# One Trainium2 core, linear attention beside a state-space convolution: two-bank PSUM tiles in neighbouring banks, position zero inside the spectrum, another issue order

## The chip, the core and the metric

The kernel runs on one core of a Trainium2 chip. Five engines work side by side, each through a queue of its own that it takes in order: PE (TensorE, matmuls and transposes; its weight loads have a row of their own, PEld), DVE (VectorE), ACT (ScalarE), POOL (GpSimd) and SP (SyncE, which here only issues DMA transfers). Work passes from engine to engine through on-chip memory: SBUF, and PSUM, into which PE writes, in eight banks of 512 float32 numbers for each of 128 partitions. The metric is the device time of one launch in microseconds (us), the median of several runs.

## The reference

Two branches on 2048 positions, 448 columns each, written side by side. The first is linear attention with 16 heads of 28 columns, in which softmax features of the projected query and key stand for the usual score matrix. The second is a state-space layer: a kernel K of length 2048 for each column, summed over 256 complex states, convolved with u, plus a skip term.

```python
# A: x [1,2048,448], wqkv [448,1344], w_phi [16,28,28], wo [448,448]
q, k, v = heads(x @ wqkv)
phi(t)  = concat(softmax(t @ w_phi), softmax(-t @ w_phi))
kv = einsum("bhsf,bhsd->bhfd", phi(k), v);  z = einsum("bhsf->bhf", phi(k))
o  = phi(q) @ kv / (phi(q) @ z + 1e-6)
a  = merge_heads(o) @ wo
# B: u [1,2048,448], A, B, C complex [448,256], log_dt, Dskip [448]
dt = exp(log_dt)
K  = einsum("dn,dnl,dn->dl", C, exp(dt * A * l), dt * B).real     # l = 0..2047
y  = irfft(rfft(u, 4096) * rfft(K, 4096))[:2048] + u * Dskip
out = concat([a, y], -1)
```

## The kernel before

The code first records 1127 operations, in the order in which a reader would write them, and then issues them in another order, which is a list of numbers, `ORDER`. An operation is a group of matmuls, or one instruction of another engine, or a DMA; `prog.add(engine, fn)` records it. A framework puts in the waits: an instruction waits for the earlier ones (in the order of issue) that touch the same memory, as far as the views that they are given tell. The stages, as recorded:

- **Loads, states, powers.** `to_states` spreads dt·A and C·B over the states by matmuls; CR is the product of C, B and dt. Tables of powers (PW) follow from exponentials, sines and squares. `flip_x` transposes x by PE into xT; `fold_weights` multiplies the key and query weights by w_phi.
- **signal_spectrum(b)**: matmuls of u with a table of constants; the result goes to DRAM (SUd) and comes back, piece by piece, for the convolution.
- **rotations, dampings, hi_tables(qt)**: for a quarter qt of the columns, arguments of sines and exponentials by matmuls into a pair of banks (`args`), then ACT, then DVE products into tables.
- **key_side**: 16 tiles of 128 positions. Each takes two projections of four matmuls (banks 4 and 5 in the code as written), two exponentials, a copy of the values (all ACT), a reduction, a reciprocal and a product (DVE), and eight matmuls that add the tile to kv and z, in a bank for each sign that stays taken through all 16 tiles (`bK`). The sets of buffers alternate between two.
- **tables(qt)**: `damp` and `far` products on DVE, and `build_k`, small matmuls that sum K over the states; K goes to DRAM (KTd) and comes back in another layout.
- **query_side(sc)**: a quarter of the positions: projections, exponentials, denominators; the scale factors go to DRAM (SCd), are read back spread over the partitions, and are multiplied into the features (EQ); then the output matmuls.
- **kernel_spectrum_pair, kernel_spectrum, conv(qt)**: the spectrum of K by matmuls with constant tables, products with the signal's spectrum on DVE (pieces of SUd come by POOL's queue into one buffer), and inverses of 36 matmuls each, whose results ACT copies out and SP stores.

Banks are handed out by a second list: the n-th `prog.take("P", ...)` gets the n-th entry of `SLOTS`, one digit for one bank, two for a pair. Of the 44 two-bank jobs, 28 have banks that are not neighbours (such as "07", "17", "26"). One of them is the argument tile of `rotations(0)` that the rows below show at 75.12: "17". A pair is read by one instruction with one view, whose step is the distance of the banks:

```python
    def two(bs, parts=128):
        return view(psum[0:parts, bs[0], 0:1], [512 * (bs[1] - bs[0]), 2], [1, D_MODEL])
```

K at position zero needs no powers: it is the sum of CR over the states. Before, matmuls of CR with a matrix of ones give that sum, the same on all partitions, and DVE adds it to DSK (the Dskip row, spread over the partitions), so that the skip term carries it.

Each engine's helper functions have one line each, which is what the profile names: `tt` L159 (DVE tensor_tensor), `smul` L171, `stt` L174, `vcopy` L177, `recip` L184, `af` L187 (ACT activation), `acopy` L190 (ACT copy), `mset` L193, `mms` L198 (matmuls), `transposes` L208, `dma` L213; the reduction of `key_side` is L592.

Of the kernel before, what the change touches and what calls it, by code (L numbers as in the profile page):

```python
# [102 lines left out]
def kernel(  # L103
# [117 lines left out]
    HM = sb(3200, [112, 4, D_HEAD + 1])  # L221
    bias_hp = sb(3440, [128, 1], F32)
# [123 lines left out]
    mset(ones, 1.0)  # L346
    dma("G", DSK, bass.AP(tensor=B_Dskip.tensor, offset=B_Dskip.offset, ap=[[0, 128], [1, D_MODEL]]))
# [5 lines left out]
    add(DSK, DSK, psum[:, bs[0], 0:D_MODEL])  # L353
# [72 lines left out]
    dma("G", HM, M_d)  # L426
    dma("G", wo, A_wo.rearrange("(c p) n -> p c n", p=112))
# [150 lines left out]
    def key_side():  # L578
        bK = prog.take("P", 6), prog.take("P", 7)
# [104 lines left out]
    def spectrum_terms(o, ft, b, rhs, sk0, m, cp):  # L684
        n = len(TERMS[b])
        items = [(o, ft[:, cp, fi, :], rhs(kt), dict(start=(k == 0), stop=(b == 0 and k == n - 1)))
                 for k, (fi, kt) in enumerate(TERMS[b])]
        if b == 1:
            items.append((o, (NEG, ident)[cp], sk0(1 - cp, m), dict(start=False, stop=True)))
        return items  # L690

    def kernel_spectrum_pair():
        tiles = {}

        def spec(m, b):
            (bk,) = prog.take("P", 4 + b)
            items = []
            for cp in range(2):
                items += spectrum_terms(
                    view(psum[:, bk, QC * cp:QC * cp + 1], [112, 2], [1, 112]), tiles[m], b,  # L700
                    lambda kt: view(KT[0][:, kt, 0:1], [672, 2], [1, 112]),
                    lambda c, k: view(SK[0][:, 0, c, k // 4, k % 4, 0:1], [3584, 2], [1, 112]), m, cp)
            mms(items)
            for g in range(2):
                acopy(SK[g][:, b, :, m // 4, m % 4, :], view(psum[:, bk, 112 * g:112 * g + 1], [QC, 2], [1, 112]))
# [7 lines left out]
    def kernel_spectrum(qt, tiles, banks):  # L713
        sk = SK[qt % 2]
        for m in range(0, 8, 2):
            for b in range(2):
                (bk,) = prog.take("P", banks[b])
                items = []
                for cp in range(2):
                    for k in range(2):  # L720
                        at = 112 * (2 * cp + k)
                        items += spectrum_terms(
                            psum[:, bk, at:at + 112], tiles[m + k], b, lambda kt: KT[qt % 2][:, kt, :],
                            lambda c, i: sk[:, 0, c, i // 4, i % 4, :], m + k, cp)
# [152 lines left out]
).split()]  # L877
SLOTS = [[int(c) for c in i] for i in (
# [33 lines left out]
```

## Time and profile before

| | |
|---|---|
| Median of 3 runs | 332.09 us (331.78 to 334.99) |
| Profiled execution, its own time | 335.36 us |
| Its span, first to last instruction | 333.4 us |
| Mean granted PE clock, as a share of full speed | 0.887 |
| DMA | 35.73 MB, 107 GB/s |

The rows below are from the one profiled execution; their times count from the span's start. In rows of the timeline the bracket holds the idle time of that engine just before the instruction, and what ended it.

### The profile page before, as it was taken

To read this page: it belongs to the slowest core of one execution; us is meant where nothing else is said; L and a number is where in the kernel's file an instruction comes from. 1 tells how busy PE (TensorE), PEld (TensorE's weight loads), DVE (VectorE), ACT (ScalarE), POOL (GpSimd) and SP (SyncE) were. 2 spreads that over 40 slices of the span, in tenths; PEclk is the share of its full clock that TensorE was granted. 3 is DMA by queue.
4 is the path that set the end of the run, shared out by engine and by line. 5 is a ranking of instruction groups with operands and counts; after the bars stand their busy time and mean duration, and the time that the engine had idled before them with its cause. 6 is when DMAs were issued, how large, how long until landed. Compare 5 with 4: busy or idle time off the path is not lost.

```text
span 333.4 us, 8578 instructions
## 1 busy us (share of the span) xinstructions
PE 249.7 (75%) x3741; PEld 186.4 (56%) x3741; DVE 267.5 (80%) x325; ACT 205.6 (62%) x340; POOL 15.6 (5%) x31
## 2 busy tenths in 40 slices
PE   2846698896699857787967577997995608979595
PEld 2735444454355544564543375647785608879595
DVE  4286958891899988696987887999996799989990
ACT  4889548887877784866847866696544421424231
POOL 7310000000000000000010000000000000100000
PEclk9975769999999985699978989999996967979899
DMA  7999105330200000042645061787509354486022
GB/s 213 253 204 237 30 2 159 111 112 0 89 23 0 0 2 1 2 89 72 122 85 234 2 168 22 157 276 247 138 4 314 74 83 168 151 210 117 0 57 58
DMA packets 51341, 35.73 MB, mean 107 GB/s; under 512 B 32008, under 2 KB 47384, under 8 KB 50920
## 3 DMA queue, kind: packets, MB, share of 16 engines
q1 hardware_dynamic: 48328, 27.90, 34.1%
q0 software_dynamic: 2976, 7.28, 7.1%
q8 instruction: 29, 0.48, 0.6%
q14 instruction: 8, 0.07, 0.1%
HBM read 26.30 MB, written 8.85 MB: 105 GB/s over the span
## 4 chain that ended last, share of the span: by engine, by line
PE 37%; DVE 28%; DMA 15%; ACT 13%; issue 4%; SPq 2%; DVEq 0%; ACTq 0%
PE psum L198 36%; DVE sbuf L159 22%; ACT sbuf L187 7%; DMA sbuf<-in_A_x_dram 5%; DMA sbuf<-in_B_C_re_dram 4%; ACT sbuf L190 4%; DMA sbuf<-SCd 4%; DVE sbuf L592 4%; SPq L213 2%; DVE sbuf L184 1%; DMA sbuf<-const 1%; ACT L187 1%; DMA SCd<-sbuf 1%; PE psum L208 0%; DVE sbuf L177 0%
## 5 line engine op out<-in xcount | busy, mean ns | idle before, releaser
L198 PE MATMUL psum<-sbuf 128*16 128x48 bf16 (+10 forms) x3632 | 237.7, 265 | 63.3 <-ACT sbuf L187 21.5
L159 DVE TENSOR_TENSOR sbuf<-sbuf 128x896 bf16<-128x896 bf16 (+13 forms) x235 | 219.5, 975 | 32.9 <-ACT sbuf L187 16.3
L198 PEld LDWEIGHTS <-sbuf 128*16 128x16 bf16 (+4 forms) x3632 | 175.3, 112 | 125.9 <-issue 70.4
L190 ACT CAST sbuf<-psum 128x448 bf16<-128x448 f32 (+4 forms) x140 | 75.4, 570 | 77.3 <-PE psum L198 70.1
L187 ACT ACTIVATE sbuf<-psum 128x448 bf16<-128x448 f32 (+4 forms) x140 | 83.9, 659 | 33.0 <-PE psum L198 31.7
L208 PE MATMUL psum<-sbuf 128*112 128x128 bf16 (+3 forms) x109 | 13.0, 305 | 16.4 <-DMA sbuf<-in_A_x_dram 7.3
L187 ACT ACTIVATE sbuf<-psum,sbuf 128x896 bf16<-128x896 f32 (+3 forms) x28 | 21.7, 807 | 2.5 <-PE psum L198 2.1
L208 PEld LDWEIGHTS <-sbuf 128*112 128x112 bf16 (+3 forms) x109 | 11.6, 207 | 17.0 <-DMA sbuf<-in_A_x_dram 8.0
L592 DVE TENSOR_REDUCE sbuf<-sbuf 128x32 f32<-128x896 bf16 x16 | 17.2, 1080 | 1.3 <-ACT sbuf L187 1.2
L177 DVE COPY sbuf<-psum 112x1024 bf16<-112x1024 bf16 (+2 forms) x16 | 7.6, 475 | 12.8 <-PE psum L208 8.6
L187 ACT ACTIVATE sbuf<-sbuf 128x896 bf16<-128x896 bf16 (+3 forms) x13 | 11.5, 901 | 8.5 <-DVE sbuf L159 7.6
L187 ACT ACT_TABLE_LOAD x11 | 14.1, 1283 | 0.9 <-PEq L896 0.7
L171 DVE TENSOR_SCALAR sbuf<-sbuf 128x3584 bf16<-128x3584 bf16 (+4 forms) x11 | 6.7, 607 | 2.1 <-PE psum L198 1.6
L184 DVE RECIPROCAL sbuf<-sbuf 128x32 bf16<-128x32 f32 (+1 forms) x20 | 7.8, 392 | 0.6
L213 POOL DMA_DIRECT2D sbuf<-SUd x4 | 2.1, 531 | 114.2 <-DVE sbuf L159 114.2
L213 POOL DMA_DIRECT2D sbuf<-const x3 | 1.7, 569 | 114.2 <-PE psum L198 114.2
L213 POOL DMA_DIRECT2D sbuf<-in_B_u_dram x8 | 6.4, 808 | 12.2 <-PE psum L208 12.2
L159 DVE TENSOR_TENSOR sbuf<-psum,sbuf 128x128 f32<-128x128 f32 (+3 forms) x10 | 4.7, 493 | 2.0 <-ACT sbuf L187 1.3
L190 ACT COPY sbuf<-psum 112x896 bf16<-112x896 bf16 x5 | 4.3, 919 | 2.3 <-PE psum L208 2.3
L190 ACT CAST sbuf<-sbuf 128x1792 bf16<-128x1792 f32 x3 | 5.1, 1691 | 0.0
L159 DVE TENSOR_TENSOR sbuf<-sbuf,psum 112x448 bf16<-112x448 bf16 (+1 forms) x2 | 1.2, 621 | 4.3 <-issue 3.4
L174 DVE SCALAR_TENSOR_TENSOR sbuf<-sbuf 128x64 f32<-128x64 f32 (+1 forms) x6 | 3.0, 506 | 0.0
(12 smaller groups left out, 9.5 us busy)
## 6 DMA issues: line engine op xcount, KB each, us to landing
sbuf<-const SPq DMA_DIRECT2D x16, 384.0 KB, 4.2
SUd<-sbuf SPq DMA_DIRECT2D x8, 448.0 KB, 4.8
sbuf<-SCd SPq DMA_DIRECT2D x16, 224.0 KB
sbuf<-SUd POOLq DMA_DIRECT2D x4, 896.0 KB, 6.2
sbuf<-const POOLq DMA_DIRECT2D x2, 1024.0 KB, 6.0
sbuf<-in_A_x_dram SPq DMA_DIRECT2D x4, 448.0 KB, 5.1
out_dram<-sbuf SPq DMA_DIRECT2D x4, 448.0 KB
sbuf<-in_B_u_dram SPq DMA_DIRECT2D x16, 112.0 KB, 4.2
```

The costliest lines, as they stand in the source:

```text
L159: prog.add("V", lambda: nc.vector.tensor_tensor(out=o, in0=a, in1=b, op=op))
L171: prog.add("V", lambda: nc.vector.tensor_scalar_mul(o, a, s))
L174: prog.add("V", lambda: nc.vector.scalar_tensor_tensor(out=o, in0=a, scalar=s, in1=b, op0=op0, op1=op1))
L177: prog.add("V", lambda: nc.vector.tensor_copy(o, a))
L184: prog.add("V", lambda: low(lambda: nc.vector.reciprocal(o, a)))
L187: prog.add("A", lambda: nc.scalar.activation(o, a, fn, **kw))
L190: prog.add("A", lambda: nc.scalar.copy(o, a))
L198: nc.tensor.matmul(o, lhsT=l, rhs=r, **kw)
L208: nc.tensor.transpose(o, i, idn)
L213: prog.add(eng, lambda: e.dma_start(out=o, in_=i))
L592: prog.add("V", lambda zk=zk, EK=EK: nc.vector.tensor_reduce(zk, EK.rearrange("p s (h f) -> p s h f", f=D_HEAD), axis=AX.X, op=ALU.add))
```

## The change

Three things change. First, both banks of a two-bank tile are now neighbours: `SLOTS` holds only the pairs 01, 12, 23, 34, 45, 56 and 67, and `key_side` takes its two accumulation banks as one such pair. Secondly, K at position zero becomes part of K's spectrum: the matrix of ones is filled with 2^-17 in place of 1, ACT copies the summed row to a new tile K0, and the real part of the spectrum for b = 0 gets one more matmul, with a table column block of ones, W[:, 0, 31, 0:128], and K0; that is 24 matmuls, 8 of them of 224 columns and 16 of 112. DVE's add goes, and DSK is loaded later on POOL's queue. Thirdly, `ORDER` and `SLOTS` are new from end to end.

```diff
+    K0 = sb(86016, [128, D_MODEL])
...
     ones = sb(212544, [128, 128])
-    mset(ones, 1.0)
-    dma("G", DSK, bass.AP(tensor=B_Dskip.tensor, offset=B_Dskip.offset, ap=[[0, 128], [1, D_MODEL]]))
+    mset(ones, 2.0 ** -17)
     bs = prog.take("P", 0)
     mms([it for qt in range(4) for it in acc(
...
-    add(DSK, DSK, psum[:, bs[0], 0:D_MODEL])
+    acopy(K0, psum[:, bs[0], 0:D_MODEL])
...
     dma("G", HM, M_d)
+    dma("G", DSK, bass.AP(tensor=B_Dskip.tensor, offset=B_Dskip.offset, ap=[[0, 128], [1, D_MODEL]]))
     dma("G", wo, A_wo.rearrange("(c p) n -> p c n", p=112))
...
     def key_side():
-        bK = prog.take("P", 6), prog.take("P", 7)
+        bk_ = prog.take("P", 6, 7)
+        bK = bk_[0:1], bk_[1:2]
...
-    def spectrum_terms(o, ft, b, rhs, sk0, m, cp):
-        n = len(TERMS[b])
-        items = [(o, ft[:, cp, fi, :], rhs(kt), dict(start=(k == 0), stop=(b == 0 and k == n - 1)))
-                 for k, (fi, kt) in enumerate(TERMS[b])]
+    def spectrum_terms(o, ft, b, rhs, k0, sk0, m, cp):
+        pairs = [(ft[:, cp, fi, :], rhs(kt)) for fi, kt in TERMS[b]]
         if b == 1:
-            items.append((o, (NEG, ident)[cp], sk0(1 - cp, m), dict(start=False, stop=True)))
-        return items
+            pairs.append(((NEG, ident)[cp], sk0(1 - cp, m)))
+        elif cp == 0:
+            pairs.append((W[:, 0, 31, 0:128], k0))
+        return acc(o, pairs)
...
 SLOTS = [[int(c) for c in i] for i in (
-    "0 12 34 0 26 34 6 0 4 3 7 0 7 0 7 0 6 5 07 07 26 34 02 34 02 67 34 67 7 0 34 26 02 02 23 67 17 23 17 17 23 "
...
+    "0 23 67 0 67 23 7 0 1 2 0 4 5 4 6 4 5 5 45 23 01 56 01 67 23 23 23 67 2 2 45 56 67 01 01 67 23 67 67 23 67 "
...
```

The new order shows best on the queues themselves. DVE where the key side begins, in the kernel before: the products of 1792 and 3584 columns make the power tables and CR's products with them, TENSOR_REDUCE, RECIPROCAL and the product of 928 belong to a key tile, and the row that reads psum is the add into DSK.

```order
L159 TENSOR_TENSOR sbuf<-psum,sbuf 128x896
L159 TENSOR_TENSOR sbuf<-sbuf 128x1792
L159 TENSOR_TENSOR sbuf<-sbuf 128x896
L159 TENSOR_TENSOR sbuf<-sbuf 128x1792
L159 TENSOR_TENSOR sbuf<-sbuf 128x3584
L592 TENSOR_REDUCE sbuf<-sbuf 128x32
L159 TENSOR_TENSOR sbuf<-sbuf 128x896
L184 RECIPROCAL sbuf<-sbuf 128x32
L159 TENSOR_TENSOR sbuf<-sbuf 128x896
L159 TENSOR_TENSOR sbuf<-sbuf,psum 128x448
L174 SCALAR_TENSOR_TENSOR sbuf<-sbuf 128x896
L159 TENSOR_TENSOR sbuf<-sbuf 128x928
```

The same place of DVE's queue after the change, from the last power tables on; COPY from psum to 112x2x4x128 is a piece of xT, and the products of 112 rows are those of B and C.

```order
L159 TENSOR_TENSOR sbuf<-sbuf 128x1792
L159 TENSOR_TENSOR sbuf<-sbuf 112x1024 x2
L159 TENSOR_TENSOR sbuf<-sbuf 128x1792
L594 TENSOR_REDUCE sbuf<-sbuf 128x32
L184 RECIPROCAL sbuf<-sbuf 128x32
L159 TENSOR_TENSOR sbuf<-sbuf 128x928
L594 TENSOR_REDUCE sbuf<-sbuf 128x32
L184 RECIPROCAL sbuf<-sbuf 128x32
L159 TENSOR_TENSOR sbuf<-sbuf 128x928
L159 TENSOR_TENSOR sbuf<-sbuf 128x1792
L177 COPY sbuf<-psum 112x2x4x128
L594 TENSOR_REDUCE sbuf<-sbuf 128x32
```

Three key tiles now stand where one stood, ahead of CR's products of 3584 columns, and there is no add that reads psum.

SP's queue, the loads of the opening, in the kernel before; in_A_x is x in four pieces, in_A_wqkv the query and key weights (896 columns) and then the value weights (448), in_B the other branch, and const 128x4096 a table of constants.

```order
L213 DMA sbuf<-in_A_x_dram 128x1792
L213 DMA sbuf<-in_A_wqkv_dram 112x4x896
L213 DMA sbuf<-in_B_A_im_dram 112x4x256
L213 DMA sbuf<-in_B_B_im_dram 112x4x256
L213 DMA sbuf<-const 128x4096
L213 DMA sbuf<-in_A_x_dram 128x1792
L213 DMA sbuf<-in_B_u_dram 64x4x448 x2
L213 DMA sbuf<-in_B_B_re_dram 112x4x256
L213 DMA sbuf<-in_B_C_im_dram 112x4x256
L213 DMA sbuf<-in_A_x_dram 128x1792 x2
L213 DMA sbuf<-in_A_wqkv_dram 112x4x448
```

The same stretch of SP's queue after the change.

```order
L213 DMA sbuf<-in_A_x_dram 128x1792
L213 DMA sbuf<-in_B_A_im_dram 112x4x256
L213 DMA sbuf<-in_A_wqkv_dram 112x4x896
L213 DMA sbuf<-in_A_x_dram 128x1792
L213 DMA sbuf<-in_B_B_im_dram 112x4x256
L213 DMA sbuf<-in_A_x_dram 128x1792
L213 DMA sbuf<-in_B_u_dram 64x4x448 x2
L213 DMA sbuf<-in_A_wqkv_dram 112x4x448
L213 DMA sbuf<-in_B_C_im_dram 112x4x256
L213 DMA sbuf<-in_B_C_re_dram 112x4x256
L213 DMA sbuf<-in_B_B_re_dram 112x4x256
```

Three pieces of x and the value weights now come ahead of three of the four loads of B and C, and the table of 4096 columns follows behind them; on POOL's queue, the four loads of w_phi, which stood ahead of all pieces of u, now stand between them.

## Rows read from the trace of the kernel before

**Rows 1.** The page: busy time of each engine, and the chain that ended last.

```profile
PE 249.7 (75%) x3741; PEld 186.4 (56%) x3741; DVE 267.5 (80%) x325; ACT 205.6 (62%) x340; POOL 15.6 (5%) x31
...
PE 37%; DVE 28%; DMA 15%; ACT 13%; issue 4%; SPq 2%; DVEq 0%; ACTq 0%
```

**Rows 2.** Stages: length, busy time of each engine, granted clock, DMA share, GB/s.

```profile
0.00:35.50 35.50, 19.70 (x153) 16.49 (x154) 20.27 (x21) 26.89 (x29) 11.14 (x21) 0.81 1.01 220
35.50:84.80 49.30, 40.71 (x256) 23.28 (x255) 34.28 (x43) 36.45 (x51) 1.20 (x4) 0.90 0.21 67
84.80:121.20 36.40, 31.27 (x219) 18.60 (x217) 34.62 (x41) 28.99 (x54) 0.00 (x0) 1.00 0.07 24
121.20:207.00 85.80, 62.76 (x1212) 44.03 (x1212) 68.38 (x97) 57.95 (x95) 1.11 (x2) 0.84 0.30 76
207.00:324.80 117.80, 90.70 (x1822) 79.53 (x1815) 109.92 (x124) 53.76 (x110) 2.12 (x4) 0.90 0.53 142
324.80:333.40 8.60, 4.61 (x94) 4.44 (x91) 0.00 (x0) 1.60 (x3) 0.00 (x0) 1.00 0.26 56
```

**Rows 3.** Waits of the whole span: total us, times, longest.

```profile
PE psum L198 <- ACT sbuf L187: 21.5, 17, 4.8
...
DVE sbuf L159 <- ACT sbuf L187: 17.6, 5, 6.6
PE psum L198 <- ACT sbuf L190: 15.6, 18, 2.3
...
DVE sbuf L159 <- DMA sbuf<-SUd: 3.2, 1, 3.2
```

**Rows 4.** Timeline from 73 to 81: start, busy time, instruction, idle before it.

```profile
75.12 0.92 ACT L187 ACTIVATE sbuf<-psum 128x896 bf16<-128x896 f32 x1 [0.28 <-PE psum L198]
...
76.08 2.44 PE L198 MATMUL psum<-sbuf 112*128 112x448 bf16 x16 [1.00 <-ACT sbuf L187]
```

**Rows 5.** DVE's timeline of the opening.

```profile
17.40 3.96 DVE L159 TENSOR_TENSOR sbuf<-sbuf 128x1792 bf16<-128x1792 f32 x2 [5.92 <-ACT sbuf L187]
...
27.39 2.30 DVE L159 TENSOR_TENSOR sbuf<-sbuf 112x1024 bf16<-112x1024 bf16 x3 [1.84 <-DMA sbuf<-in_B_C_im_dram]
...
44.33 1.08 DVE L592 TENSOR_REDUCE sbuf<-sbuf 128x32 f32<-128x896 bf16 x1
...
50.10 0.62 DVE L159 TENSOR_TENSOR sbuf<-sbuf,psum 128x448 bf16<-128x448 bf16 x1 [3.42 <-issue]
```

**Rows 6.** DMA, 0 to 40 us: busy tenths in 40 slices; issues, us to landing.

```profile
DMA  0069999999999999999999999999999999500000
...
sbuf<-in_B_u_dram POOLq DMA_DIRECT2D x8, 112.0 KB, 13.1
...
sbuf<-in_A_w_phi_dram POOLq DMA_DIRECT2D x4, 6.1 KB, 4.9
```

**Rows 7.** SP's queue from 138 to 160: issues of transfers.

```profile
141.26 0.34 SPq L213 DMA_DIRECT2D SCd<-sbuf  x1
144.85 1.70 SPq L213 DMA_DIRECT2D sbuf<-SCd  x4
```

**Rows 8.** DVE's timeline from 140 to 172.

```profile
152.88 2.36 DVE L159 TENSOR_TENSOR sbuf<-sbuf 112x2048 bf16<-112x2048 bf16 x2 [2.40 <-DMA sbuf<-SCd]
```

**Rows 9.** Timeline from 322 to the end.

```profile
320.30 4.48 DVE L159 TENSOR_TENSOR sbuf<-sbuf 128x3584 bf16<-128x3584 bf16 x6
...
329.50 0.53 ACT L190 CAST sbuf<-psum 128x448 bf16<-128x448 f32 x1 [1.29 <-PE psum L198]
```

**Rows 10.** Groups by shape: busy us, mean ns, idle before.

```profile
L198 PE MATMUL psum<-sbuf 128*128 128x112 bf16 x808 | 47.3, 226 | 11.8 <-ACT sbuf L187 5.8 <-DVE sbuf L159 3.5 <-issue 2.0
...
L190 ACT CAST sbuf<-psum 128x448 bf16<-128x448 f32 x64 | 33.4, 538 | 42.0 <-PE psum L198 35.1 <-DVE sbuf L159 4.5 <-issue 1.8
```

**Rows 11.** Two stretches of 20 us, columns as in rows 2.

```profile
20.00:40.00 20.00, 13.32 (x108) 10.98 (x109) 16.15 (x19) 15.43 (x15) 1.88 (x3) 0.59 0.83 161
...
100.00:120.00 20.00, 18.27 (x137) 11.54 (x135) 18.93 (x26) 15.79 (x32) 0.00 (x0) 1.00 0.00 1
```

More of the change, by code (lines that the diff above doesn't have):

```diff
@@ L700, in spec @@
                     view(psum[:, bk, QC * cp:QC * cp + 1], [112, 2], [1, 112]), tiles[m], b,
-                    lambda kt: view(KT[0][:, kt, 0:1], [672, 2], [1, 112]),
+                    lambda kt: view(KT[0][:, kt, 0:1], [672, 2], [1, 112]), view(K0[:, 0:1], [112, 2], [1, 112]),
                     lambda c, k: view(SK[0][:, 0, c, k // 4, k % 4, 0:1], [3584, 2], [1, 112]), m, cp)
@@ L723, in kernel_spectrum @@
                             psum[:, bk, at:at + 112], tiles[m + k], b, lambda kt: KT[qt % 2][:, kt, :],
+                            K0[:, 112 * qt:112 * qt + 112],
                             lambda c, i: sk[:, 0, c, i // 4, i % 4, :], m + k, cp)
```

94 rows, old and new, of tables (ORDER, SLOTS) are left out of this document.

## The prediction

> **What bounds the kernel now.** I read the page's busy shares and chain first, then each engine's busy time by stage, then who waits for whom, and last the places in the timeline where those waits stand. DVE is busy 267.5 of 333.4 us, PE 249.7, ACT 205.6, and the chain that ended last passes through all of them: PE 37%, DVE 28%, DMA 15%, ACT 13% [rows 1]. No engine is full over the whole span; the kernel loses time where engines hand work over. The stages show where [rows 2]. DVE sits idle 15.2 us of the first 35.5 (loads and power tables), 15.0 of the next 49.3 (first part of the key side), only 1.8 of the 36.4 in which the key side ends, 17.4 of 85.8 (tables and query side), 7.9 of 117.8 (spectra and convolution), and all of the last 8.6. That is 65.9 us; a better order or fewer waits can take back that and no more, unless it also cuts DVE's work.
>
> Some of the handovers are between instructions that share no data. At 75.12 ACT starts on the two-bank argument tile of `rotations(0)`, which lies in banks 1 and 7. It started, after 0.28 us of idle time, when signal_spectrum's matmuls ended, though these write banks 2 and 3; and PE's value projection of key tile 2, into bank 4, stood 1.00 us until ACT was through [rows 4]. The view of banks 1 and 7 is one stepped pattern, and what lies between them is waited for as if it were read. 28 of the 44 two-bank jobs had such a pair. Matching each wait of the trace with the banks in `SLOTS`, I count 47 in which the engine that ended last shares no bank with the one that waits, 57.6 us of local idle time, 38.6 of it ACT's and 16.6 PE's. Most of that is no loss of the kernel: what counts is what reaches DVE, for which the grouped waits give 17.6 us behind ACT, while PE stands 21.5 and 15.6 us behind ACT [rows 3].
>
> **The change part by part.**
>
> *Opening, to 35.5 us.* The DMA engines are full from 2 to 35 us [rows 6], and nothing is loaded less, so the loads' own waits stay: at DVE 5.92 us before 17.40 and 1.84 us before 27.39 [rows 5]. DVE's first key-tile reduction stands at 44.33 there [rows 5]; the new order puts x and the value weights ahead on SP's queue and the reductions right behind the power tables, so they fill some of the 15.2. I take 11 us of idle as left, between 7.8 (these two waits alone) and 15.2: −4.2.
>
> On POOL's queue the four loads of w_phi go between pieces of u. Here they took a median of 4.9 us and the eight pieces 13.1 [rows 6], so the last may land 8.2 us later; PE's folding of weights waits for it, and the first projection of a key tile for that. With x only partly there by then I take nothing for it, 8.2 as the far end. The rows say that transfers of this size take their time while all engines are full. The Trainium skill, page "DMA: Bandwidth & Descriptors", section "Issuing engines are not separate DMA queues", says that transfers share the 16 engines whoever issues them, and that several issuers save only issuing time; by it the new places on POOL's queue would change less than the 8.2, and the sum not at all.
>
> *Key side.* Of 85.7 us DVE is idle 16.8 [rows 2]. The false handovers lie here above all: `rotations`, `dampings`, `signal_spectrum` and `hi_tables` use pairs between the key tiles. In the second half, where DVE has table work between tiles, it is idle 5% (1.78 of 36.40). If that holds for the whole 85.7, 4.2 are left; I take 5.0, so −11.8 (ends: 0 and −15). About 18 us of table work that stood ahead of the last key tile now stands behind it; it is moved, not removed, and makes the middle denser.
>
> *Position zero.* DVE's add into DSK goes: 0.62 us, after 3.42 idle that lie in the key side's 15.0 already [rows 5]. So −0.6. In its place ACT copies 128x448 from PSUM, 0.538 us a piece [rows 10]; ACT is idle 12.9 us of that stretch [rows 2], so zero, 0.5 at most. PE gets 24 matmuls: 16 of 112 columns at 226 ns, and 8 of 224 which I price alike from below and at twice that from above: 5.4 to 7.2 us [rows 10]. PE is idle 27.1 us in the last working stage [rows 2]; without that cover all would count. I take 0.7, an eighth, as reaching DVE. DSK's load moves behind others and is needed only for the final adds: zero.
>
> *Middle, 121.2 to 207.* DVE waits here for chains that go around it. One is the store of the query side's factors to DRAM and its reload: store issued at 141.26, loads issued from 144.85, DVE's multiply at 152.88 [rows 7, 8], 11.6 us. In the new order the DVE work that stands between is 9 to 11.7 us for each of the four, so most is covered, with 7 to 9 us of idle time left for the four with shortfalls, queueing behind other transfers, and the transposes ahead of them; squares on ACT add 1 to 3. Of 17.4 I keep 11.4: −6.0 (ends −2 and −9).
>
> *Convolution.* One buffer takes each next piece of signal spectrum. DVE stood 3.2 us for one of them [rows 3]. It remains one buffer, so 1.5 us twice, and 2.4 for tables of constants: 5.4 of 7.9 stay, −2.5 (ends 0 and −4).
>
> *Tail.* DVE ends at 324.78, when PE still has three inverses of 36 matmuls in its queue, one every 1.8 us (ACT stands idle 1.29 before it copies one out in 0.53); ACT's last copy is at 329.50 and takes 0.53, and the last store ends the span at 333.40 [rows 9]. In the new order one inverse depends on, and stands behind, DVE's last instruction: 1.8 + 0.53 + 3.4 (from 330.03 to 333.40) = 5.7; with 0.2 of handovers 5.9, not 8.6: −2.7 (ends −3.6 and 0, as PE may still be behind).
>
> **Sum:** −4.2 −11.8 −0.6 +0.7 −6.0 −2.5 −2.7 = −27.1. The profiled execution took 335.36, so 308.3; the median of the timed runs lies 3.27 below it (332.09): 305.
>
> **The rivals.**
>
> *B, DVE alone decides.* If interleaving keeps it fed, its busy time, 267.5 − 0.6 = 266.9, plus loads 7.8, tail 5.9 and the two DMA waits of [rows 3, 8] (3.2 + 2.4 = 5.6) give a span of 286; less 1.3, which is how the median stands to the span, 285. For it: DVE at 95% in one stage already. Against: PE and ACT each have over 200 us and their chains must then never come late.
>
> *C, the key side stays an interlock.* Its −11.8 falls away, the rest holds: 317. For it: two projections, two exponentials, a copy, a reduction, a reciprocal, a multiply and eight matmuls follow each other through three engines with two sets of buffers, which the change leaves alone. Against: the second half already does it at 95%. A pair now has only seven places, so it may wait truly for a bank where it waited falsely before. The Trainium skill, page "Perfetto Trace Analysis", section "Matmuls", says that independent groups of matmuls should go round different banks, so that one is emptied while the next is filled; by it fewer places for pairs cost time, and the outcome would be this one. No row separates the two, as both look like PE waiting for ACT.
>
> *Nothing reaches the path.* The waits removed were off it, and a new order brings waits of its own as long: 332, give or take 3.3.
>
> *D, slower: the clock.* PE's granted clock in 20 to 40 us was 0.59, near the lower of its two levels (1.2 of 2.4 GHz), after a stretch in which PE waited for loads; from 100 to 120 it was 1.00 [rows 11]. If short matmul groups separated by DVE-paced gaps hold it at 0.59 through the key side, the 72.0 us that PE was busy there at 0.94 (mean of [rows 2]) become 115; that stage ends at 35.5 + 115 = 150.5 in place of 121.2, and +29 against the −4.2 −0.6 +0.7 −6.0 −2.5 −2.7 of the rest gives 346. It decides from a mean clock of about 0.65, at which PE's time there is 104 and eats what the rest brings. Against: the new order has fewer waits between PE's groups, and 0.90 and 1.00 were held with more. The Trainium skill, page "TensorE: Matmul & The Clock Gate", section "Part 1: The HAM clock gate", says the slow state is the default and activity lifts it; the trace agrees in its 0.59 and 1.00, and whether gaps of the new kind suffice no row shows.
>
> **How the numbers follow.** Forecast 0.52 (296 to 313), B 0.14 (285 to 296), C 0.20 (313 to 324), nothing 0.06, D 0.08. Leaving out D, nothing and the lower half of B gives 290 to 324 for the range. A measurement of this kernel tells about 1% (3.3 us) from no change: faster 0.86, same 0.06, slower 0.08.
>
> **What would show it.** In the profile after: the first key reduction near 33 us instead of 44.33, the last 10 us or more earlier than before; DVE over 90% busy in the key side; PE's waits for ACT well under 37 us together; DVE's last instruction within 6 us of the end; no wait of 3 us for SUd. The prediction is wrong if the granted clock of the key side falls under 0.8, if DVE's waits there stay near 30%, or if the four reload chains leave gaps over 3 us each.

## The result: 307.49 us, a ratio of 0.9245

The changed kernel takes 307.49 us (median of four runs, 307.09 to 309.14) beside 333.54 for the kernel before (331.78 to 343.97, of which 343.97 was disturbed and is left out of the ratio): 0.9245, with a 95% interval of 0.917 to 0.9319. The forecast was 305, with a range of 290 to 324. The profiled execution has a span of 305.1 us in place of 333.4.

The page of the changed kernel, answering to [rows 1]:

```profile
PE 240.7 (79%) x3765; PEld 180.1 (59%) x3765; DVE 263.4 (86%) x324; ACT 201.5 (66%) x341; POOL 15.6 (5%) x31
```

Its stages, answering to [rows 2] (length; busy time of PE, PEld, DVE, ACT, POOL; granted clock; DMA share; GB/s). They are cut at the first reduction of a key tile, the end of the key side, the end of the query side, and DVE's last instruction.

```profile
0.00:45.10 45.10, 20.83 (x130) 14.17 (x131) 23.71 (x27) 26.82 (x30) 10.53 (x21) 0.92 0.74 160
45.10:93.70 48.60, 44.09 (x393) 29.39 (x391) 46.63 (x70) 44.31 (x75) 1.84 (x4) 1.00 0.17 50
93.70:188.00 94.30, 79.60 (x1278) 52.64 (x1278) 88.20 (x101) 72.51 (x116) 0.00 (x0) 0.93 0.27 66
188.00:298.60 110.60, 93.16 (x1910) 81.02 (x1909) 104.81 (x130) 56.79 (x119) 3.19 (x6) 0.95 0.66 176
298.60:305.10 6.50, 3.02 (x62) 2.86 (x59) 0.01 (x1) 1.08 (x3) 0.00 (x0) 1.00 0.32 71
```

Subtract DVE's busy time from each length: it is idle 21.4, 2.0, 6.1, 5.8 and 6.5 us, 41.7 in all, where it was idle 65.9. Taken against [rows 2], opening and key side together fall from 32.0 to 23.4 (−8.7), the middle from 17.4 to 6.1 (−11.3), the convolution from 7.9 to 5.8 (−2.1) and the tail from 8.6 to 6.5 (−2.1). That is −24.2; DVE's busy time falls by 4.1, and the two make the 28.3 us of the span.

The waits, answering to [rows 3] (total, times, longest):

```profile
DVE sbuf L159 <- ACT sbuf L187: 12.3, 5, 4.1
...
PE psum L198 <- ACT sbuf L190: 9.5, 11, 4.1
PE psum L198 <- ACT sbuf L187: 7.5, 8, 2.4
...
DVE sbuf L594 <- ACT sbuf L187: 4.1, 1, 4.1
```

PE's standing behind ACT falls from 37.1 us to 17.0. What is left on DVE lies early: 4.1 of it directly ahead of the first key reduction, which begins at 45.09 and not at the 33 that the prediction named.

### The profile page after: what moved, and what is told of

It reads as the page before. It is cut to its first block, busy times and chain, and to the rows that moved or that the text cites. A ratio compares the mean times of both kernels' runs of the same rounds, so it can differ in the third digit from the quotient of the medians.

```text
span 305.1 us, 8613 instructions
## 1 busy us (share of the span) xinstructions
PE 240.7 (79%) x3765; PEld 180.1 (59%) x3765; DVE 263.4 (86%) x324; ACT 201.5 (66%) x341; POOL 15.6 (5%) x31
## 5 line engine op out<-in xcount | busy, mean ns | idle before, releaser
L198 PE MATMUL psum<-sbuf 128*16 128x48 bf16 (+8 forms) x3656 | 231.0, 262 | 44.4 <-DVE sbuf L159 15.7
L159 DVE TENSOR_TENSOR sbuf<-sbuf 128x896 bf16<-128x896 bf16 (+14 forms) x235 | 218.0, 974 | 17.1 <-ACT sbuf L187 8.2
L198 PEld LDWEIGHTS <-sbuf 128*16 128x16 bf16 (+4 forms) x3656 | 170.0, 110 | 102.4 <-issue 52.6
L187 ACT ACTIVATE sbuf<-psum 128x448 bf16<-128x448 f32 (+4 forms) x140 | 82.1, 677 | 15.5 <-PE psum L198 11.1
L208 PE MATMUL psum<-sbuf 128*112 128x128 bf16 (+3 forms) x109 | 11.9, 273 | 16.5 <-DMA sbuf<-in_A_wqkv_dram 5.4
L208 PEld LDWEIGHTS <-sbuf 128*112 128x112 bf16 (+3 forms) x109 | 10.5, 177 | 19.0 <-DMA sbuf<-in_A_x_dram 6.0
L187 ACT ACT_TABLE_LOAD x11 | 14.1, 1283 | 2.5 <-DVE sbuf L159 1.6
L193 POOL MEMSET sbuf<- 128x16 bf16 (+3 forms) x6 | 1.5, 257 | 48.2 <-DVE sbuf L159 47.9
```

The lines of the kernel that those rows point to most:

```text
L159: prog.add("V", lambda: nc.vector.tensor_tensor(out=o, in0=a, in1=b, op=op))
L187: prog.add("A", lambda: nc.scalar.activation(o, a, fn, **kw))
L193: prog.add("G", lambda: nc.gpsimd.memset(o, v))
L198: nc.tensor.matmul(o, lhsT=l, rhs=r, **kw)
L208: nc.tensor.transpose(o, i, idn)
```

## The experiments

All times are medians of at least four runs; each has the kernel before on the same chip beside it, at a median of 334.96 to 336.90 us, so the ratios compare better than times from different chips. A ratio is given with its 95% interval.

**The changed kernel with its banks renamed, so that pairs lie apart** (bank 0 becomes 2, and so on; one line of each table shown):

```diff
 SLOTS = [[int(c) for c in i] for i in (
-    "0 23 67 0 67 23 7 0 1 2 0 4 5 4 6 4 5 5 45 23 01 56 01 67 23 23 23 67 2 2 45 56 67 01 01 67 23 67 67 23 67 "
+    "2 16 07 0 07 16 7 0 5 1 2 3 4 3 0 3 4 4 34 16 25 04 25 07 16 16 16 07 1 1 34 04 07 25 25 07 16 07 07 16 07 36 0 "
```

> The changed kernel with its eight banks renamed, nothing else: pairs 01, 12, 23, 34, 45, 56, 67 become 2 and 5, 1 and 5, 1 and 6, 3 and 6, 3 and 4, 0 and 4, 0 and 7, so that most pairs are read with a step of three to seven banks again. Order, instructions and true dependences stay. Theory 'waits' (the false handovers carried the gain): half of the 26 us or more comes back, 320 us or above, and waits of ACT for PE and of PE for ACT rise again by more than 10 us in the key side. Theory 'order' (the new issue order carried it, and leaves slack for the false waits): at most 312 us. Between the two, 314 to 318, I would call both.

Measured: 374.44 us, a ratio of 1.116 (1.107 to 1.125) to the kernel before; 67 us more than the changed kernel, for new numbers of banks alone. Its stages, cut at the same instructions as above:

```profile
0.00:50.80 50.80, 21.31 (x130) 14.60 (x131) 23.82 (x27) 27.15 (x30) 10.53 (x21) 1.00 0.66 142
50.80:120.50 69.70, 53.19 (x393) 32.53 (x390) 47.72 (x71) 44.41 (x73) 1.84 (x4) 0.83 0.12 35
120.50:247.00 126.50, 87.56 (x1278) 55.11 (x1277) 88.70 (x101) 76.22 (x117) 0.00 (x0) 0.76 0.19 49
247.00:364.50 117.50, 95.61 (x1912) 80.85 (x1910) 104.82 (x130) 57.60 (x119) 3.18 (x6) 0.93 0.62 167
364.50:371.00 6.50, 3.04 (x62) 2.88 (x59) 0.02 (x1) 1.06 (x2) 0.00 (x0) 1.00 0.19 43
```

DVE does the same work, and is idle 22.0 us in the key side and 37.8 in the middle, where it was 2.0 and 6.1. The convolution, whose matmuls go to single banks, loses less: 12.7 us idle against 5.8. One place in its timeline between 70 and 73 us shows the wait:

```profile
71.12 1.17 ACT L187 ACTIVATE sbuf<-psum 128x896 bf16<-128x896 f32 x2 [0.96 <-PE psum L198]
72.09 1.30 PE L198 MATMUL psum<-sbuf 128*112 128x116 bf16 x9 [1.01 <-ACT sbuf L187]
```

ACT's first instruction at 71.12 reads the argument tile of `dampings(0)`, here in banks 0 and 7; it ends at 72.04. PE's matmuls at 72.09 add key tile 3 to kv, in banks 2 and 5. They share nothing with what ACT reads; their banks lie between. The instruction itself is not slower for its step: the 128x896 activation takes 932 ns there, and 960 in the changed kernel. What grew is the waiting. The renamed pairs also lie further apart than those of the kernel before (165 banks in between in all, against 103), so the 67 us are not what the change took away.

**The same with the numbers mirrored** (bank b becomes 7 − b, all pairs stay neighbours):

```diff
-    "0 23 67 0 67 23 7 0 1 2 0 4 5 4 6 4 5 5 45 23 01 56 01 67 23 23 23 67 2 2 45 56 67 01 01 67 23 67 67 23 67 "
+    "7 45 01 0 01 45 0 0 6 5 7 3 2 3 1 3 2 2 23 45 67 12 67 01 45 45 45 01 5 5 23 12 01 67 67 01 45 01 01 45 01 34 0 "
```

> The changed kernel with bank b renamed to 7 - b, nothing else: all 45 pairs remain neighbours. If what cost time in the run with pairs apart was the banks between the two of a pair, nothing changes here: 306.5 to 308.5 us. If new numbers for banks cost time by themselves (another engine's neighbour, a place that the planner had fitted): above 310.

Measured: 307.61 us. New numbers cost nothing while pairs stay neighbours.

**The same with one bank between the two of most pairs:**

```diff
-    "0 23 67 0 67 23 7 0 1 2 0 4 5 4 6 4 5 5 45 23 01 56 01 67 23 23 23 67 2 2 45 56 67 01 01 67 23 67 67 23 67 "
+    "0 46 13 0 13 46 1 0 2 4 0 7 5 7 3 7 5 5 57 46 02 35 02 13 46 46 46 13 4 4 57 35 13 02 02 13 46 13 13 46 13 67 0 "
```

> The changed kernel with its banks renamed so that 40 of the 45 pairs have exactly one bank between them (13, 46, 35, 02, 57, 24) and 5 have none; with pairs apart, 41 pairs had 2 to 6 between them, some 125 in all. If each bank in between is a chance of a false wait, a third of the added 67 us: 320 to 340. If a stepped view costs alike whatever its step (the engine reads it slower): 360 to 375. If one bank in between is rarely in use at that time: 308 to 315.

Measured: 322.82 us (320.88 to 326.36), about 15 more than the changed kernel. With pairs apart there were 165 banks in between (14 pairs with six, 10 with four, 10 with two, 7 with three; the expectation's 125 was miscounted), here 40. A share of 40 in 165 of the 67 us is 16, and 15 came. A price for the step as such, which would have left the time at 360 or more, is ruled out; a price for what lies in between fits, by this one point.

**The pairs apart, but read bank by bank.** Every instruction of ACT and DVE that reads two banks with a step is issued as two, each of one bank:

```diff
+    def banks2(a):
+        return a.tensor.name.startswith("psum") and list(a.ap[1])[1] == 2 and list(a.ap[1])[0] % 512 == 0
+
+    def each(a, *rest):
+        if not banks2(a):
+            return [(a,) + rest]
+        return [tuple(v[:, k] for v in (a,) + rest) for k in range(2)]
...
-        prog.add("A", lambda: nc.scalar.activation(o, a, fn, **kw))
+        prog.add("A", lambda: [nc.scalar.activation(o_, a_, fn, **kw) for a_, o_ in each(a, o)])
```

(`acopy` and `tt` likewise.)

> The kernel with pairs apart, in which every instruction that reads two banks with a step is two instructions that read one bank each; banks, order and matmuls as there. Theory 'view' (the wait is for what lies between the two banks of one view): the added time goes, less some 11 us of ACT's (about 68 instructions, 2 x 0.55 in place of 0.93 to 0.96), of which ACT's idle time covers much: 308 to 318 us. Theory 'place' (those banks are really in use at those times, by neighbours that the renaming made): the time stays above 355.

Measured: 307.43 us (306.85 to 308.85), all 67 us back. ACT issues 429 instructions in place of 341 (88 more; the 68 in the expectation was too few).

**The changed kernel with the same split,** neighbouring pairs as they are:

> The changed kernel with the same split, as the price of the split by itself: 307 to 315 us. By theory 'view' it equals the split kernel with pairs apart within 2 us, since with one-bank reads it makes no difference which banks they are; by theory 'place' it is 40 us faster than that one.

Measured: 307.41 us (305.53 to 310.92), the same as with pairs apart, and the same as without the split. Read bank by bank, it makes no difference which banks a pair has; and ACT's added 6 us of busy time (207.5 against 201.5) cost nothing that can be measured.

**The kernel before, its order kept, with all pairs in neighbouring banks** (banks planned anew):

```diff
-    "0 12 34 0 26 34 6 0 4 3 7 0 7 0 7 0 6 5 07 07 26 34 02 34 02 67 34 67 7 0 34 26 02 02 23 67 17 23 17 17 23 "
+    "0 67 45 0 23 45 1 0 2 0 0 1 0 1 0 1 3 2 01 01 23 45 23 45 23 01 45 01 0 1 45 23 23 23 23 01 01 23 01 01 23 01 0 "
```

> The kernel before with its own issue order and code, and banks planned anew so that all 44 pairs lie in neighbouring banks, with hardly any job put on a bank that is still in use. Theory 'waits': 316 to 322 us, as DVE's idle time in the key side (15.0 and 1.8 us) falls by about 12. Theory 'order': 328 to 333 us, since the instructions stand in the queues as before and DVE's idle time there stays above 12.

Measured: 316.34 us, a ratio of 0.940 (0.934 to 0.947).

**The kernel before, its order and banks kept, split as above:**

> The kernel before, with its own order, banks and code, except that every instruction that reads two banks with a step is two instructions that read one bank each. Theory 'view': as much as neighbouring banks brought in that order (316.3 us), 313 to 320, with DVE's idle time in the first part of the key side (15.0) and in the middle (17.6) falling by about 9 each. If the gain there came from the banks planned anew (fewer true conflicts) and not from the views: 326 to 335.

Measured: 312.72 us, a ratio of 0.938 (0.925 to 0.951) to the kernel before on that chip; none of its runs took more than 314.63 us, and none of the kernel before less than 331.88. Its stages are cut at the instructions of [rows 2]:

```profile
0.00:37.30 37.30, 19.76 (x158) 16.79 (x159) 20.18 (x23) 27.63 (x47) 11.14 (x21) 0.82 1.04 208
37.30:76.80 39.50, 36.04 (x252) 20.92 (x252) 33.71 (x46) 38.25 (x79) 1.20 (x4) 1.00 0.27 86
76.80:113.40 36.60, 31.03 (x222) 18.81 (x222) 34.78 (x41) 29.33 (x59) 0.00 (x0) 1.00 0.07 22
113.40:186.40 73.00, 58.84 (x1212) 41.47 (x1211) 67.57 (x96) 58.98 (x121) 1.11 (x2) 0.94 0.36 93
186.40:300.90 114.50, 88.19 (x1810) 77.47 (x1809) 109.62 (x124) 54.94 (x123) 2.12 (x4) 0.92 0.53 144
300.90:309.20 8.30, 4.80 (x98) 4.63 (x95) 0.04 (x1) 1.65 (x4) 0.00 (x0) 0.92 0.27 57
```

DVE's idle time, stage by stage against [rows 2]: 17.1 (15.2), 5.8 (15.0), 1.8 (1.8), 5.4 (17.4), 4.9 (7.9), 8.3 (8.6). So 9 us come from the first half of the key side, 12 from the middle and 3 from the convolution, while the opening holds 2 more, with no instruction moved. The run with planned neighbours has the same pattern (18.2, 5.6, 1.9, 7.7, 4.6, 8.6). With fewer waits the granted clock of PE rose too, from 0.90 to 1.00 in the first half of the key side and from 0.84 to 0.94 in the middle; what of the gain is the clock's, no run separates.

**Position zero, undone in the changed kernel:**

```diff
-    mset(ones, 2.0 ** -17)
+    mset(ones, 1.0)
...
-    acopy(K0, psum[:, bs[0], 0:D_MODEL])
+    add(DSK, DSK, psum[:, bs[0], 0:D_MODEL])
...
-        elif cp == 0:
-            pairs.append((W[:, 0, 31, 0:128], k0))
```

(`ORDER` also issues DSK's load early again.)

> The changed kernel with position zero as it was before: the matrix of ones holds 1, DVE adds the row to DSK, DSK is loaded early on POOL's queue, and the 24 added matmuls are gone. If position zero is worth what the prediction's sum says (0.6 less on DVE, 0.7 more for matmuls): 306.5 to 308.5, no difference. If the add was a stall of 3 to 4 us wherever it stands: 310 to 312. If the 24 matmuls lie on the path: 303 to 305.

Measured: 307.56 us: no difference.

**Position zero alone, put into the kernel before** (the opposite edit, with the order and banks of before):

> The kernel before, its order and its banks, with position zero in the spectrum: ones hold 2^-17, ACT copies the row to K0, 24 matmuls are added, DVE's add is gone. By the prediction's sum, 0.6 less and 0.7 more: 330 to 335, no difference from before. If the 3.4 us of idle time ahead of the add were its own: 4 us less, 328 to 330.

Measured: 336.84 us, a ratio of 1.008 (1.002 to 1.014) to the kernel before: nothing gained, perhaps 1 to 5 us lost. The 3.4 us of idle time ahead of the add [rows 5] were not the add's own; in the kernel before with its reads split, above, the add begins at 47.86 with no idle time ahead of it.

**Six steps of the opening moved in the changed kernel** (37 and 38 are the copy and the subtraction that make TH, 104 to 107 the folding of the key weights, 209 the first value projection, 64 a sine; job 13, a piece of xT, goes from bank 4 to bank 0):

```diff
-    "80 81 69 59 58 60 67 68 57 100 101 25 12 18 22 78 21 109 92 93 28 79 209 9 94 19 71 72 106 40 95 164 73 37 "
-    "38 64 7 61 104 107 105 8 42 212 108 236 65 62 27 208 89 226 210 217 218 221 90 39 219 220 41 110 163 66 111 "
+    "81 69 59 58 60 67 68 57 100 101 25 12 18 22 78 21 109 92 93 28 79 9 94 19 71 37 38 106 104 209 107 105 64 72 40 "
+    "95 164 73 7 61 8 42 212 108 236 65 62 27 208 89 226 210 217 218 221 90 39 219 220 41 110 163 66 111 88 222 223 "
...
-    "0 23 67 0 67 23 7 0 1 2 0 4 5 4 6 4 5 5 45 23 01 56 01 67 23 23 23 67 2 2 45 56 67 01 01 67 23 67 67 23 67 "
+    "0 23 67 0 67 23 7 0 1 2 0 4 5 0 6 4 5 5 45 23 01 56 01 67 23 23 23 67 2 2 45 56 67 01 01 67 23 67 67 23 67 34 0 "
```

> The changed kernel with six steps of the opening moved: the copy and the subtraction that make the two parts of TH come ahead of the last low power's products on DVE, so that ACT's sines do not stand 6.3 us behind that subtraction, and the folding matmuls of the key weights come ahead of the first value projection, which waits 3.2 us for its weights. Theory 'queues' (the opening gained nothing because ACT and PE stood in their queues behind instructions that were not ready): the first key reduction moves from 45.1 to 39 to 41 us and the time to 301 to 304. Theory 'loads' (DMA sets the opening, whatever the order): the first reduction stays within 1 us of 45.1 and the time within 306.5 to 308.5.

Measured: 299.61 us, 7.9 less than the changed kernel; the fastest of all. The first key reduction begins at 37.58. Its first two stages, cut at the same instructions as those of the changed kernel:

```profile
0.00:37.60 37.60, 20.04 (x134) 14.31 (x135) 23.37 (x27) 27.36 (x31) 10.53 (x21) 1.00 0.88 189
37.60:86.20 48.60, 43.60 (x388) 29.00 (x387) 46.63 (x71) 43.58 (x75) 1.84 (x4) 1.00 0.18 52
```

The key side is the same 48.6 us, only begun 7.5 us earlier. My expectation put PE's stand of 3.2 us ahead of the value projection down to its weights; the trace of the changed kernel says otherwise, below.

**Two of the six alone** (37 and 38):

```diff
-    "80 81 69 59 58 60 67 68 57 100 101 25 12 18 22 78 21 109 92 93 28 79 209 9 94 19 71 72 106 40 95 164 73 37 "
-    "38 64 7 61 104 107 105 8 42 212 108 236 65 62 27 208 89 226 210 217 218 221 90 39 219 220 41 110 163 66 111 "
+    "81 69 59 58 60 67 68 57 100 101 25 12 18 22 78 21 109 92 93 28 79 209 9 94 19 71 37 38 72 106 40 95 164 73 64 7 "
+    "61 104 107 105 8 42 212 108 236 65 62 27 208 89 226 210 217 218 221 90 39 219 220 41 110 163 66 111 88 222 223 "
```

> The changed kernel with two of the six steps of the reordered opening moved: the copy and the subtraction that make TH come ahead of the last low power's products on DVE; the folding matmuls stay behind the value projection. If ACT's stand of 6.3 us behind that subtraction held the opening: 301 to 303, most of the 7.9 us that all six brought. If PE's stand of 3.2 us for the value weights held it, or both must go: 305 to 308.

Measured: 301.08 us, 6.4 of the 7.9. The first key reduction begins at 39.65.

**The loads of w_phi ahead of those of u, in the changed kernel** (16 to 19 are the four loads):

```diff
-    "2 0 1 4 3 29 30 31 32 33 45 20 46 34 44 15 17 11 82 5 24 16 36 35 83 43 14 6 10 54 55 26 84 85 23 102 56 103 "
-    "80 81 69 59 58 60 67 68 57 100 101 25 12 18 22 78 21 109 92 93 28 79 209 9 94 19 71 72 106 40 95 164 73 37 "
+    "2 0 1 4 3 29 30 31 32 33 45 20 46 34 44 15 17 16 18 19 11 82 5 24 36 35 83 43 14 6 10 54 55 26 84 85 23 102 56 "
+    "103 80 81 69 59 58 60 67 68 57 100 101 25 12 22 78 21 109 92 93 28 79 209 9 94 71 72 106 40 95 164 73 37 38 64 "
```

> The changed kernel with the four loads of w_phi back ahead of the pieces of u on POOL's queue. In the run of the changed kernel they landed between 5 and 22.3 us, and the folding matmuls that need the last began at 31.2. If the opening is held by ACT's and PE's queues: no difference, 306.5 to 308.5. If by w_phi, as the far end of the prediction's sum had it: 2 to 8 us less.

Measured: 305.07 us (302.45 to 306.43), at the edge of the two: 2.4 less by the medians, with intervals that overlap a little (0.903 to 0.920 against 0.917 to 0.932). Their landing falls from a median of 12.3 to 5.2 us, but the first key reduction moves by 0.5 us only, to 44.6. Whether the rest is more than the spread between chips stays open.

## Why the prediction came out, point by point

**The bound and the false handovers: right, and shown.** The step that a wait between instructions without common data costs real time holds: renaming costs 67 us, reading bank by bank takes all of it away again, and in the kernel before the split alone makes it 6.2% faster. I had counted 57.6 us of local idle time and kept most of it off the path; 21 to 24 us of it reached the end (the 333.4 us span against 312.4 and 309.2 for the two runs in the old order).

**Where they lie: half right.** I put them in the key side "above all", at −11.8. The runs in the old order show 9.2 and 9.3 us there, near it, and 10 to 12 in the middle, which the prediction gave to something else.

**The middle, −6.0 by cover for the reload chains: the wrong cause, and half the size.** It measured −11.3. In the old order, with the chains of stores and reloads standing where they stood, views alone brought 10 to 12 us there. The reload itself was never more than a small part: of the kernel before's 17.4 us, DVE waited 2.4 for it [rows 8]; with planned neighbours it still waited 2.6, with the split 1.4, and in the changed kernel 0.6 in the middle and 2.1 in all. DVE's waits in the middle, first of the kernel before, then of the changed one (total, times, longest):

```profile
DVE sbuf L177 <- PE psum L208: 4.2, 2, 3.1
DVE sbuf L159 <- ACT sbuf L187: 3.8, 2, 2.4
DVE sbuf L159 <- DMA sbuf<-SCd: 2.4, 1, 2.4
DVE sbuf L177 <- ACT sbuf L187: 1.9, 2, 1.1
DVE sbuf L177 <- PE psum L198: 1.9, 2, 1.1
```

```profile
DVE sbuf L159 <- ACT sbuf L187: 3.3, 1, 3.3
DVE sbuf L159 <- DMA sbuf<-SCd: 0.6, 1, 0.6
```

Most of what DVE waited for in the middle was work of ACT and PE; as the split alone took it away, that work had been held behind reads of other banks.

**The opening, −4.2 with the first reduction near 33: wrong.** DVE is idle 15.2 us of the first 35.5 in both kernels, and the first reduction came at 45.09. Counted up to the first reduction, the opening even lost: before, DVE was busy 28.6 of the 44.3 us ahead of it and idle 15.7, now 21.4. The step that failed is "the reductions right behind the power tables, so they fill some of the 15.2": standing early in DVE's queue is of use only if ACT has made the exponentials by then. ACT's timeline of the changed kernel shows what held it:

```profile
26.94 0.89 ACT L190 CAST sbuf<-psum 128x896 bf16<-128x896 f32 x1
34.13 1.90 ACT L187 ACTIVATE sbuf<-psum,sbuf 128x896 f32<-128x896 f32 x2 [6.30 <-DVE sbuf L159]
...
41.01 0.54 ACT L187 ACTIVATE sbuf<-psum 128x448 bf16<-128x448 f32 x1
```

and DVE's and PE's:

```profile
33.01 1.08 DVE L159 TENSOR_TENSOR sbuf<-psum,sbuf 128x896 bf16<-128x896 f32 x1
...
38.92 2.03 DVE L159 TENSOR_TENSOR sbuf<-sbuf 128x1792 bf16<-128x1792 f32 x1 [2.02 <-ACT sbuf L187]
45.09 1.08 DVE L594 TENSOR_REDUCE sbuf<-sbuf 128x32 f32<-128x896 bf16 x1 [4.14 <-ACT sbuf L187]
```

```profile
24.67 1.01 PE L208 MATMUL psum<-sbuf 128*112 128x128 bf16 x8 [2.43 <-ACT sbuf L190]
28.84 1.67 PE L198 MATMUL psum<-sbuf 112*128 112x448 bf16 x4 [3.16 <-DVE sbuf L177]
```

The sines at 34.13 read the same two banks as DVE's subtraction (start 33.01, 1.08 long); they begin when it ends, and behind them in ACT's queue stand the copies of the folded weights, and the first exponentials at 41.01. The subtraction had been ready since ACT's copy of 26.94 was done, and stood behind five other instructions of DVE. The value projection at 28.84 waited for DVE's copy of the piece of xT that it reads, out of the bank that it writes, and not for a load. Moving the two steps that make TH gave 6.4 us and the first reduction at 39.65; with all six it stands at 37.58.

**Key side, interlock or not: right.** DVE is busy 46.63 of 48.6 us, 96%, as the second half of before had it; rival C is out. I had read the rule cited for it, of the Trainium skill, page "Perfetto Trace Analysis", section "Matmuls", that independent groups should go round different banks, as speaking against fewer places for pairs. The runs show no price for that: in the old order, with the false waits gone either way, the ratio is 0.940 (0.934 to 0.947) with seven places and 0.938 (0.925 to 0.951) with the old ones. From the first reduction on, DVE was idle 16.3 us of the key side before and 2.0 now, more than the −11.8, but the opening's loss takes part of it back: the two terms together were put at −16.0 and measured −8.7.

**Position zero, −0.6 and +0.7: right** as a sum, nothing in the changed kernel (307.56 against 307.49), and no gain in the one before. The two terms one by one are too small for these runs to show.

**Convolution −2.5 and tail −2.7: right in size,** −2.1 each. DVE's wait for SUd is 1.2 us where it was 3.2 [rows 3]. In the tail PE had 62 matmuls left to run after DVE's last instruction, more than the 36 of the one inverse that I had counted.

**DVE's busy time, −0.6: too small by 3.5.** It fell by 4.1; see the last section.

That the sum came out so close (28.3 of span against 27.1) is luck: the middle's and the busy time's surplus (5.3 and 3.5) made up for the opening and key side's shortfall (7.3). Of the signs that the prediction named, four came (the last key reduction over 10 us earlier, DVE over 90% busy in the key side, PE's waits for ACT well under 37 us, no wait of 3 us for SUd) and two did not (the first reduction near 33, DVE's end within 6 us of the end: it was 6.5).

**The rivals.** B (285): DVE's idle time is 41.7 us, not 19; the opening alone holds 21.4, and the reordered run shows that 7 of those were not loads but queues. D: the granted clock is 1.00 in the key side, where its two halves had 0.90 and 1.00 [rows 2]; no slow key side came. What did fall is the clock of the run with pairs apart, to 0.83 in the key side and 0.76 in the middle: PE is busy 9.1 and 8.0 us longer there for the same matmuls, which is part of the 67 us.

**How much is the new order?** With both read bank by bank, the old order takes 312.72 and the new one 307.41, 5 us; with neighbours in both, 316.34 and 307.49, it is 9. These are times from different chips; by the ratios to the kernel before it is about 7 and 5. The order moved hundreds of instructions; the views of 44 tiles, at 21 to 24 us, were worth two to four times as much.

## What to carry to other kernels

Here the waits were put in from views, and a strided view over two far places waited for all that lay between them: in such a case look in the trace for waits whose two ends share no buffer, and either place the two side by side or split the instruction, which was free here while ACT had time to spare. Before an early place in a queue is counted as a gain, ask what makes its input, and follow that engine's queue head back; a reader of the same bank that stands late on another engine can hold it. Put back one part at a time: two parts that look alike in a diff were worth over 20 us and nothing.

## What the runs showed of the hardware that was not expected

DVE's busy time falls when it waits less, with the same instructions but for the add of 0.6 us: 267.5 us before, 265.8 there with planned neighbours; 265.1 in the changed kernel with pairs apart, 263.4 with neighbours. Rows of the changed kernel's timeline, DVE alone, show an instruction begin before the one ahead has ended:

```profile
46.21 0.35 DVE L184 RECIPROCAL sbuf<-sbuf 128x32 bf16<-128x32 f32 x1
46.67 0.64 DVE L159 TENSOR_TENSOR sbuf<-sbuf 128x928 bf16<-128x928 bf16 x1
47.23 1.08 DVE L594 TENSOR_REDUCE sbuf<-sbuf 128x32 f32<-128x896 bf16 x1
```

The product at 46.67 takes 0.64 and would end at 47.31; the reduction begins at 47.23. The reciprocal at 46.21 needs the reduction that began at 45.09 and took 1.08, and starts 0.04 after its end. In the whole trace 166 instructions of DVE begin before the one ahead has ended in the kernel before, and 201 in the changed one, by a median of 0.08 us and 14.1 and 16.8 us in all. So 2.7 of the 4.1 us come from these overlaps and 0.6 from the add. A sum of durations misses it.

Two engines that only read the same bank were kept apart as well: ACT's sines waited for DVE's subtraction though both only read those two banks. Whether the chip needs that or only the framework orders it, no run here tells.
